# Opening loads of a two-layer SiLU kernel: the first w1 slab on one queue, the x tiles in smaller transposes

## The chip, the cores and the metric

The kernel runs on one core of one Trainium2 chip. The metric is the device time of one execution in microseconds (us); the number that counts is the median of several runs. Below, TensorE is PE in the profile (PEld is its weight load), ScalarE is ACT, VectorE is DVE, GpSimd is POOL and SyncE is SP. SP and ACT each have a queue on which they issue DMAs (SPq and ACTq).

## What is computed

`x` is 2048 x 640, `w1` is 640 x 1728, `w2` is 1728 x 640, all bf16:

```
h = silu(x @ w1)      # 2048 x 1728
out = h @ w2          # 2048 x 640
```

## The kernel before

The contraction of the first product runs over 640 = 5 tiles of 128 (`DT`, index `k`). The 1728 columns of w1 are 13 full tiles of 128 and a tail of 64 (index `ft`). The 2048 rows of x are four chunks of 512 (`SCH`, index `c`). x is brought in by DMA transposes (`turned`, line 90, and line 163), so that the contraction lies on the partitions. `xT[:, k, ...]` is contraction tile k of x, called x tile k below for chunk 0; `w1s[:, k, ...]` is the matching part of w1, and its first 1024 columns (eight tiles of 128, 256 KB) are called slab k.

A product of 128 w1 columns with 512 rows of x is issued as two matmuls of 64 columns each (`step`, line 183), which run side by side; such a pair is the unit counted below.

**Chunk 0** is ordered so that PE can begin with little data. PE takes x tile 0 with the eight column tiles of slab 0, one PSUM bank for each (eight pairs, "sweep 0"), then x tile 1 with slab 1, and so on to sweep 4, after which the eight banks are complete. Sweep k waits for slab k and x tile k (`opening`, line 197, and line 208). Then come the remaining five column tiles of chunk 0 (loads `ld_rest` and `ld_rest2`), five pairs each, and then chunks 1 to 3, each waiting for five transposes on one semaphore (`ld_xc`). The second product follows.

**Ahead of the first real matmul** PE runs matmuls on a zeroed tile `z` (`first_dummies`, line 135): thirteen of 128 columns by 256 and one pair of 64 columns by 256.

**The order of the DMAs** is written out by hand. `early` puts an instruction ahead of the kernel's opening barrier, on its engine, in the order of the calls. Before the change that order is:

- SPq: x tiles 0 and 1 in one transpose (line 123); columns 640 to 1023 of slab 0 (`ld_w1b`, line 148, 96 KB); slab 1; slab 2; x tile 2; slab 3; x tiles 3 and 4 in one transpose; slab 4; `ld_rest` (320 KB); `ld_rest2` (560 KB); then, in the body, fifteen transposes for chunks 1 to 3 and the loads of w2.
- ACTq: columns 0 to 639 of slab 0 (line 124, 160 KB), then the table load and a small activation (`warm_up`).

In sweep 0, PE waits for x tile 0 and ACT's part of slab 0, and ahead of the sixth column tile (`ft == NA`) for `ld_w1b`.

Of the kernel before, what the change touches and what calls it, by code (L numbers as in the profile page):

```python
# [9 lines left out]
def bass_standalone__dense_activation_silu__prompt_kernel(  # L10
# [13 lines left out]
    P = 128  # L24
    NB = 8
    BANK = 512
    DT = D // P
    FT = F // P
    FL = F - FT * P
    SCH = 512  # L30
# [8 lines left out]
    pe, act, dve, pool, sp = nc.tensor, nc.scalar, nc.vector, nc.gpsimd, nc.sync  # L39

    with ExitStack() as es:
# [18 lines left out]
        def sem(name):  # L60
            s = es.enter_context(nc.semaphore(name))
            count[s.name if hasattr(s, "name") else name] = 0
            return [s, 0]

        def tick(ins, s, n=1):
            ins.then_inc(s[0], n)
            s[1] += n
            return (s, s[1])

        def wait(eng, *points):  # L70
            for pt in points:
                if pt is None:
                    continue
                s, v = pt
                key = (id(eng), id(s))
                if seen.get(key, 0) < v:
                    eng.wait_ge(s[0], v)
                    seen[key] = v
# [6 lines left out]
        def load(eng, out_ap, in_ap):  # L85
            s = sem(f"s_ld{n_dma[0]}")
            n_dma[0] += 1
            return tick(eng.dma_start(out=out_ap, in_=in_ap), s, 16)

        def turned(c0, c1, k0, k1):  # L90
            s = sem(f"s_tr{n_dma[0]}")
            n_dma[0] += 1
            return tick(sp.dma_start_transpose(
                out=xT[:, k0:k1, c0:c1], in_=xf[c0:c1, k0 * P:k1 * P]), s, 16)

        ET = mybir.EngineType

        def early(emit, engine, arrived=True):
            n = len(nc.main_func.blocks[0].instructions)
            r = emit()  # L100
            lst = nc.main_func.blocks[0].instructions
            new = lst[n:]
            del lst[n:]
            at = next(
                i for i, ins in enumerate(lst)
                if ins.opcode == ("EventSemaphore" if arrived else "Drain") and ins.engine == engine
            )
            lst[at:at] = new
            return r
# [2 lines left out]
        w2_v = w2[0:F0, :].rearrange("(ft p) d -> p ft d", p=P)  # L112

        NO = NB
        NA = 5
        CO = NO * P

        def slab(eng, k, f0=0, f1=NO):
            return load(eng, w1s[:, k, f0 * P:f1 * P], w1_v[:, k, f0 * P:f1 * P])

        ld_w1 = {}
        ld_t = {}
        ld_t[0] = ld_t[1] = early(lambda: turned(0, SCH, 0, 2), ET.SP, False)
        ld_w1[0] = early(lambda: slab(act, 0, 0, NA), ET.Activation, False)
        p_z = early(lambda: tick(dve.memset(z[:, :], 0.0), s_dve), ET.DVE, False)  # L125

        bank_free = [None] * NB
# [1 line left out]
        def dummies(n, w):  # L129
            for _ in range(n):  # L130
                for c0 in range(0, P, w):
                    pe.matmul(ps[c0:c0 + w, 3, 0:HB], lhsT=z[:, 0:w], rhs=z[:, :],  # L132
                              start=True, stop=True)

        def first_dummies():
            wait(pe, p_z)
            dummies(13, P)
            dummies(1, HC)

        p_warm = early(lambda: tick(pool.memset(warm[:, :], 0.0), s_pool), ET.Pool, False)  # L140
# [4 lines left out]

        early(warm_up, ET.Activation, False)

        ld_w1b = early(lambda: slab(sp, 0, NA, NO), ET.SP, False)
        ld_w1[1] = early(lambda: slab(sp, 1), ET.SP, False)
        ld_w1[2] = early(lambda: slab(sp, 2), ET.SP, False)  # L150
        ld_t[2] = early(lambda: turned(0, SCH, 2, 3), ET.SP, False)
        ld_w1[3] = early(lambda: slab(sp, 3), ET.SP, False)
        ld_t[3] = ld_t[4] = early(lambda: turned(0, SCH, 3, DT), ET.SP, False)
        ld_w1[4] = early(lambda: slab(sp, 4), ET.SP, False)
        CM = CO + 2 * P
        ld_rest = early(lambda: load(sp, w1s[:, :, CO:CM], w1_v[:, :, CO:CM]), ET.SP, False)
# [32 lines left out]
        def part(k, ft, c0, c1, start=False, stop=False):  # L189
            return step(ft, k, ft, c0, c1, start, stop)  # L190

        def sweep(k, c0, c1, *waits):
            wait(pe, *waits)
            for ft in range(NO):
                part(k, ft, c0, c1)

        def opening():
            first_dummies()
            wait(pe, ld_t[0], ld_w1[0])
            for ft in range(NO):  # L200
                if ft == NA:
                    wait(pe, ld_w1b)
                part(0, ft, 0, SCH, start=True)
            for k in range(1, DT - 1):
                sweep(k, 0, SCH, ld_w1[k], ld_t[k])

        early(opening, ET.PE)
        wait(pe, ld_w1[4], ld_t[4])
        for ft in range(NO):
# [198 lines left out]
```

## Time and profile before

| what | value |
|---|---|
| median of 3 runs | 124.7 us (124.55 to 125.05) |
| span of the profiled execution, first to last instruction | 123.8 us |
| PE busy | 121.3 us, 98% of the span |
| ACT busy | 38.8 us, 31% |
| DVE busy | 6.9 us, 6% |
| first dummy matmul, from the span's start | 0.39 us |
| first real matmul | 3.82 us |
| granted TensorE clock, mean | 1.000 |
| DMA moved | 10.42 MB, mean 84 GB/s |

The profiled execution has no separate device time on record; its span is its own time, and the runs' median lies 0.9 us above it, for what comes before the first and after the last instruction. All times inside an execution are counted from the span's start. An issue is the time in which the queue's engine hands a DMA over; a DMA has landed when its semaphore has its full count.

### The profile page before, as it was taken

Reading aid. Unit: us, or ns where it says so; the run is one execution under the profiler, and the core shown is the slowest. Engines: PE = TensorE matmul, PEld = TensorE weight load, DVE = VectorE, ACT = ScalarE, POOL = GpSimd, SP = SyncE. Lnnn points to the kernel's source line nnn. Section 1 sums busy time; section 2 is a strip of 40 time slices with the busy share of each in tenths; the row PEclk is TensorE's granted clock in tenths of the full one; section 3 lists DMA queues with packets and bytes.
Section 4 is the critical chain, followed back from the end, with each engine's and each line's share of the span. In section 5 each row is a group of like instructions: output and inputs, shape, how many; then the busy total and the mean of one; then the engine's idle time right before and its main releaser. Section 6 shows DMA issues by size and latency. Waiting matters only on the chain.

```text
span 123.8 us, 2298 instructions
## 1 busy us (share of the span) xinstructions
PE 121.3 (98%) x1056; PEld 58.9 (48%) x1057; DVE 6.9 (6%) x11; ACT 38.8 (31%) x67; POOL 0.3 (0%) x5
## 2 busy tenths in 40 slices
PE   8999999999999999999999999999999999999993
PEld 5345545545545545545544444444444444444452
DVE  0000000000000000000000022002200300222001
ACT  4000985555555555555530011001100200110110
POOL 0000000000000000000000000000000000000000
DMA  6999974554894000000000004302200220023112
GB/s 138 239 246 331 138 86 91 100 77 107 214 394 157 0 0 0 3 5 0 0 0 5 0 0 101 74 0 105 107 0 5 106 106 0 5 106 116 53 66 82
DMA packets 19625, 10.42 MB, mean 84 GB/s; under 512 B 13728, under 2 KB 19104, under 8 KB 19616
## 3 DMA queue, kind: packets, MB, share of 16 engines
q1 hardware_dynamic: 19472, 10.11, 34.1%
q10 hardware_dynamic: 144, 0.16, 0.6%
q8 instruction: 8, 0.13, 0.5%
q14 instruction: 1, 0.01, 0.0%
HBM read 4.51 MB, written 2.62 MB: 58 GB/s over the span
## 4 chain that ended last, share of the span: by engine, by line
PE 95%; DMA 3%; ACT 0%; issue 0%
PE ps L175 95%; DMA xT<-in_x_dram 3%; ACT o_sb L256 0%
## 5 line engine op out<-in xcount | busy, mean ns | idle before, releaser
L175 PE MATMUL ps<-xT,w1s 128*64 128x512 bf16 x540 | 59.6, 384 | 0.1
L175 PE MATMUL ps<-w2s,hT 64*128 64x512 bf16 (+3 forms) x376 | 46.0, 369 | 0.2 <-issue 0.2
L175 PEld LDWEIGHTS ps<-xT,w1s 128*64 128x64 bf16 x540 | 30.0, 111 | 29.6 <-issue 1.2
L179 ACT ACTIVATE hT<-ps 128x512 bf16<-128x512 f32 x52 | 30.0, 607 | 29.9 <-PE ps L175 29.9
L175 PEld LDWEIGHTS ps<-w2s,hT 64*128 64x128 bf16 (+1 forms) x377 | 21.0, 95 | 24.2 <-issue 0.2
L256 ACT CAST o_sb<-ps 128x512 bf16<-128x512 f32 (+1 forms) x9 | 5.0, 551 | 41.5 <-PE ps L175 41.5
L175 PE MATMUL ps<-hT,w2s 64*128 64x512 bf16 x104 | 11.7, 376 | 0.0
L175 PEld LDWEIGHTS ps<-hT,w2s 64*128 64x128 bf16 x104 | 5.0, 94 | 6.3 <-issue 0.4
L254 DVE CAST o_sb<-ps 128x512 bf16<-128x512 f32 (+1 forms) x8 | 5.4, 675 | 40.5 <-PE ps L175 40.5
L254 DVE CAST oT<-ps 128x512 bf16<-128x512 f32 x2 | 1.4, 692 | 74.2 <-PE ps L175 74.2
L256 ACT CAST oT<-ps 128x512 bf16<-128x512 f32 x2 | 1.2, 586 | 10.6 <-PE ps L175 10.6
L132 PE MATMUL ps<-z 128*128 128x256 bf16 (+1 forms) x15 | 3.3, 419 | 0.4 <-DVE z L125 0.4
L175 PE MATMUL ps<-w2t,hTt 64*128 64x512 bf16 (+2 forms) x17 | 2.9, 363 | 0.0
L132 PEld LDWEIGHTS ps<-z 128*128 128x128 bf16 (+1 forms) x15 | 1.9, 142 | 1.5 <-issue 0.4
L179 ACT ACTIVATE hTt<-ps 128x512 bf16<-128x512 f32 x2 | 1.2, 598 | 1.0 <-PE ps L175 1.0
L144 ACT ACT_TABLE_LOAD x1 | 1.3, 1283 | 0.5 <-issue 0.5
L175 PEld LDWEIGHTS ps<-w2t,hTt 64*128 64x128 bf16 x17 | 0.9, 94 | 1.1
L175 PE MATMUL ps<-hTt,w2t 64*128 64x512 bf16 x4 | 0.8, 376 | 0.0
L175 PEld LDWEIGHTS ps<-hTt,w2t 64*128 64x128 bf16 x4 | 0.2, 94 | 0.2
L144 ACT ACTIVATE warm<-warm 128x32 f32<-128x32 f32 x1 | 0.2, 229 | 0.0
L125 DVE MEMSET z<- 128x128 uint32 x1 | 0.2, 165 | 0.2 <-issue 0.2
L140 POOL MEMSET warm<- 128x32 f32 x1 | 0.1, 125 | 0.0
(4 smaller groups left out, 0.4 us busy)
## 6 DMA issues: line engine op xcount, KB each, us to landing
out_dram<-o_sb SPq DMA_DIRECT2D x15, 160.0 KB, 1.8
w2s<-in_w_dram SPq DMA_DIRECT2D x1, 1120.0 KB, 6.1
w1s<-in_w_dram SPq DMA_DIRECT2D x4, 256.0 KB, 4.1
w2s<-in_w_dram SPq DMA_DIRECT2D x1, 960.0 KB, 8.2
w1s<-in_w_dram SPq DMA_DIRECT2D x1, 560.0 KB, 7.0
w1s<-in_w_dram SPq DMA_DIRECT2D x1, 320.0 KB, 5.8
xT<-in_x_dram SPq DMA_TRANSPOSE x18, 3.7
w1s<-in_w_dram ACTq DMA_DIRECT2D x1, 160.0 KB, 2.7
```

What stands on the lines that cost most here:

```text
L125: p_z = early(lambda: tick(dve.memset(z[:, :], 0.0), s_dve), ET.DVE, False)
L132: pe.matmul(ps[c0:c0 + w, 3, 0:HB], lhsT=z[:, 0:w], rhs=z[:, :], start=True, stop=True)
L140: p_warm = early(lambda: tick(pool.memset(warm[:, :], 0.0), s_pool), ET.Pool, False)
L144: act.activation(out=warm[:, :], in_=warm[:, :], func=ACT.Silu)
L175: return pe.matmul(o, lhsT=l, rhs=r, start=start, stop=stop, skip_group_check=shared)
L179: r = tick(act.activation(out=out_ap, in_=in_ap, func=ACT.Silu), s_act)
L254: r = tick(dve.tensor_copy(out=out_ap, in_=in_ap), s_dve)
L256: r = tick(act.copy(out=out_ap, in_=in_ap), s_act)
```

## The change

ACT loads the whole of slab 0, so `ld_w1b`, its wait and `NA` are gone. The first transpose on SPq brings x tile 0 alone; x tile 1 has a transpose of its own, behind slab 1, followed by that of x tile 2, which so moves ahead of slab 2. Slab 3 follows slab 2 directly; the rest keeps its order. There are eleven dummies of 128 columns instead of thirteen.

```
-        ld_t[0] = ld_t[1] = early(lambda: turned(0, SCH, 0, 2), ET.SP, False)
-        ld_w1[0] = early(lambda: slab(act, 0, 0, NA), ET.Activation, False)
+        ld_t[0] = early(lambda: turned(0, SCH, 0, 1), ET.SP, False)
+        ld_w1[0] = early(lambda: slab(act, 0), ET.Activation, False)
...
-            dummies(13, P)
+            dummies(11, P)
             dummies(1, HC)
...
-        ld_w1b = early(lambda: slab(sp, 0, NA, NO), ET.SP, False)
         ld_w1[1] = early(lambda: slab(sp, 1), ET.SP, False)
+        ld_t[1] = early(lambda: turned(0, SCH, 1, 2), ET.SP, False)
+        ld_t[2] = early(lambda: turned(0, SCH, 2, 3), ET.SP, False)
         ld_w1[2] = early(lambda: slab(sp, 2), ET.SP, False)
-        ld_t[2] = early(lambda: turned(0, SCH, 2, 3), ET.SP, False)
         ld_w1[3] = early(lambda: slab(sp, 3), ET.SP, False)
-        ld_t[3] = ld_t[4] = early(lambda: turned(0, SCH, 3, DT), ET.SP, False)
+        ld_t[3] = ld_t[4] = early(lambda: turned(0, SCH, 3, 5), ET.SP, False)
         ld_w1[4] = early(lambda: slab(sp, 4), ET.SP, False)
...
             for ft in range(NO):
-                if ft == NA:
-                    wait(pe, ld_w1b)
                 part(0, ft, 0, SCH, start=True)
```

More of the change, by code (lines that the diff above doesn't have):

```diff
@@ L114, in bass_standalone__dense_activation_silu__prompt_kernel @@
         NO = NB
-        NA = 5
         CO = NO * P
```

## The prediction

> **What bounds the kernel now.** I read the page first, then the chain of waits in order of time, then the timeline of the first 9 us, then each opening DMA by itself. The page:
>
> ```profile
> span 123.8 us, 2298 instructions
> ...
> PE 121.3 (98%) x1056; PEld 58.9 (48%) x1057; DVE 6.9 (6%) x11; ACT 38.8 (31%) x67; POOL 0.3 (0%) x5
> ...
> PE 95%; DMA 3%; ACT 0%; issue 0%
> PE ps L175 95%; DMA xT<-in_x_dram 3%; ACT o_sb L256 0%
> ```
>
> PE is the bound; the one other thing on the chain is a load of x. The chain in order of time:
>
> ```profile
> 0.00 3.78 DMA xT<-in_x_dram
> 3.78 0.04 issue
> 3.82 106.78 PE ps L175 x706
> ```
>
> The first transpose (x tiles 0 and 1) lands at 3.78, the first real matmul starts at 3.82, and from there PE is not interrupted for 106.78 us. So the change can win only by starting before 3.82, and lose only by putting a hole into what follows. The weight loads and SP's queue:
>
> ```profile
> 3.27 0.13 PEld L132 LDWEIGHTS ps<-z 128*64 128x64 bf16 x2 [0.41 <-issue]
> 3.82 0.18 PEld L175 LDWEIGHTS ps<-xT,w1s 128*64 128x64 bf16 x4 [0.42 <-DMA xT<-in_x_dram]
> 4.25 0.18 PEld L175 LDWEIGHTS ps<-xT,w1s 128*64 128x64 bf16 x2 [0.25 <-issue]
> ...
> 5.53 0.18 PEld L175 LDWEIGHTS ps<-xT,w1s 128*64 128x64 bf16 x2 [0.25 <-DMA w1s<-in_w_dram]
> 5.96 0.18 PEld L175 LDWEIGHTS ps<-xT,w1s 128*64 128x64 bf16 x2 [0.25 <-issue]
> 6.30 2.27 PEld L175 LDWEIGHTS ps<-xT,w1s 128*64 128x64 bf16 x22 [0.17 <-issue]
> ```
> ```profile
> 0.00 1.33 SPq L93 DMA_TRANSPOSE xT<-in_x_dram  x1
> 1.39 1.54 SPq L88 DMA_DIRECT2D w1s<-in_w_dram  x3
> 2.97 1.16 SPq L93 DMA_TRANSPOSE xT<-in_x_dram  x1
> 4.17 0.58 SPq L88 DMA_DIRECT2D w1s<-in_w_dram  x1
> 4.79 1.24 SPq L93 DMA_TRANSPOSE xT<-in_x_dram  x1
> 6.07 1.62 SPq L88 DMA_DIRECT2D w1s<-in_w_dram  x3
> 8.09 9.67 SPq L163 DMA_TRANSPOSE xT<-in_x_dram  x6
> ```
>
> The first rows show the pace: pairs start 0.427 apart up to 5.96, 0.34 apart once, then 0.216 (the timeline of 7 to 8 us: five pairs in 1.08). PE doubles its pace at about 6.22 (a gap of 0.343 is 0.26 us at the slow pace and the rest at the fast one), although the granted clock reads 1.00 in every stretch. The wait for the second part of slab 0 at 5.53 costs nothing: the idle 0.25 before it is that of its neighbours. Sweep 0 ends at 6.73 and each later sweep takes 8 x 0.216 = 1.73: sweeps 1 to 4 start at 6.73, 8.46, 10.19, 11.91, the remaining tiles at 13.64, chunk 1 at 13.64 + 25 x 0.216 = 19.04.
>
> **What an earlier start is worth.** A start earlier by d, with the pace doubling at the same 6.22, puts d/0.427 more pairs ahead of that point, which save 0.216 each behind it: 0.505 d. This halving is my largest choice. The trace has one doubling, 5.83 after the first dummy (0.39) and 2.40 after the first real pair; what it is tied to isn't shown. I keep it at 6.22, since PE's first dummy stays where it is; the other ties are rivals.
>
> **Part 1: when the first pair can start.**
> - x tile 0 alone: the upper bound is the two-tile transpose, 3.78. The nearest rows of one tile: 2.8 from issue to landing (the one issued at 16.49), 2.4 for the o_sb transpose from oT, 4.2 with a full queue (x tile 2). It shares its time with slab 0; I take 3.2, between 2.8 and 3.78 and nearer the lone one, as nothing is ahead of it on its queue.
> - slab 0 on ACT: issued at 0.12, the 160 KB landed 2.7 later, at 2.8. The 96 KB more, at the 248 GB/s that moved between 2 and 3 us, are 0.4: 3.2. Bounds: 2.8, and 0.12 + 3.9 = 4.0 (a 256 KB slab on SP).
> - Dummies: eleven at 0.213 (eight start from 0.39 to 1.86) end the last pair of dummies at 3.49 - 0.43 = 3.06, ahead of the data, so they hold nothing up.
>
> Start: 3.25, which is 0.57 earlier; worth 0.505 x 0.57 = **0.29 us**. Bounds of the start: 3.06 (dummies; 0.38 us) to 4.0 (0.09 us lost).
>
> **Part 2: the queue behind it.** SP loses one issue (0.61, from 1.39 to 2.00) and gains one transpose (1.20 from issue to next issue for x tile 2, 1.31 in the chain from 16.49). Going down the queue with these rows: x tile 0 at 0.00, slab 1 at 1.31, x tile 1 at 1.92, x tile 2 at 3.12, slab 2 at 4.37, slab 3 at 4.98, x tiles 3 and 4 at 5.47, slab 4 at 6.75, the rest loads at 7.37 and 7.85, chunk 1 from 8.77 (was 8.09: 0.68 later). With before's time from issue to landing for the same kind of DMA (slabs 3.9 to 4.5, x tile 2 4.2, x tiles 3 and 4 4.4, rest 5.8 and 7.0), against the need with a start at 3.25 and no hole:
>
> | needed by | need | lands by those rows |
> |---|---|---|
> | sweep 1: slab 1, x tile 1 | 6.44 | 5.2, 6.1 |
> | sweep 2: slab 2, x tile 2 | 8.17 | 8.5, 7.3 |
> | sweep 3: slab 3, x tile 3 | 9.90 | 9.1, 9.9 |
> | sweep 4: slab 4 | 11.62 | 11.25 |
> | rest, rest2 | 13.35, 15.5 | 13.2, 14.85 |
> | chunk 1 (last transpose 14.57 + 3.4 before) | 18.75 | 18.7 |
>
> Only slab 2 is late, by 0.3, in the worst reading: it was issued at 2.49 and is now at 4.37, behind both transposes. The latencies are those of a queue with a backlog. Less is ahead of it now than the rows suggest: up to slab 2 the DMAs have 896 KB to move against 864 before, but 1.9 us more to do so. Its lower bound is the 2.7 of ACT's load, 7.1; the middle of 7.1 and 8.5 is 7.8, and I take no hole. If all else fits as well, the cost of part 2 is 0, with 0.3 as its upper bound; below 0 it can't be, as PE had no hole after 3.82. ACT's longer issue is hidden: its first real activation is at 12.34. The wait removed at 5.53 was worth nothing.
>
> **Sum.** 0.29 less than the span of 123.8: 123.5, and with the 0.9 around it **124.4** (0.24% less). A measurement of this kernel can tell about 0.5%, or 0.6 us, from no change (its three runs lie 0.5 apart), so this forecast is within it.
>
> **Rivals.**
> - **A, the two loads hold each other up.** Before the first pair, 256 + 128 = 384 KB must land instead of 160 + 256 = 416. If bytes set the time, the stretch from 1.0 (first movement) to 3.78 shrinks by 32/416, 0.2 us: start 3.6, gain 0.505 x 0.2 = 0.1, 124.6. For it: the busiest early second shows 248 GB/s, well under the 347 between 10 and 11 us. Against: the transpose's small packets, now half as many, were last to land, one microsecond after slab 0's part. [...]
> - **B, the order gives it back.** Slab 2 lands at 8.5 as by the rows above: a hole of 0.3 and the gain is gone, 124.7. It would need a landing after 9.1 to lose 0.6.
> - **C, the pace doubles 2.40 after the first real pair.** Then it doubles at 5.65 and the whole 0.57 is won: 124.1. For it: 3 us of dummies had not doubled the pace. Against: there is no reason in the trace that zeros count less.
> - **D, the pace doubles later (slower).** The dummies now end at 3.06. Before, PE was idle 0.33 us (3.49 to 3.82) between them and the first pair, and the pace still doubled. If the data come after 3.4, the idle time is longer than that, and if it makes the warm-up begin anew, the 5.83 count from the first pair: with a start at 3.6, 9.43 instead of 6.22. That costs 3.21 x 0.495 less the 0.1 of A, 1.5 us: 126.2. A smaller delay costs half of itself. At a start of 3.25 the idle time is 0.19, shorter than before, which speaks against it. [...]
>
> **How the numbers follow.** Forecast 0.44, A 0.12, B 0.14, C 0.12, D 0.18. The forecast itself spreads by some 0.3 either way (the runs' spread, bounds of the start): 124.1 to 124.7. Faster by over 0.5% (below 124.1): 0.15 of the forecast, half of C and a little of the others, 0.23. Slower by over 0.5% (above 125.3): nearly all of D, and 0.06 of a hole in sweep 2 or chunk 1 beyond the rows, 0.24. Within 0.5%: 0.53. The range from 123.8 to 125.8 takes in A, B, C and the smaller delays of D, and leaves out some 0.07 below and 0.12 above.
>
> **What the profile after would show.** Right: the chain starts with a DMA that lands at 3.1 to 3.4, pairs 0.427 apart from there to about 6.2, then 0.216 with no idle time of PEld up to chunk 1. A: a start near 3.6, with slab 0 or x tile 0 named. B: an idle time before sweep 2, put down to w1s. C: the doubling near 5.65. D: slow pairs beyond 6.7, and a longer idle time ahead of the first. The prediction is wrong if x tile 0 lands no sooner than 3.7, or if the doubling moves by more than half a microsecond.

## The result and the profile after

| | before | after |
|---|---|---|
| median of 8 runs | 124.53 us (124.29 to 125.05) | 125.15 us (124.92 to 125.34) |
| ratio, 95% interval | | 1.0053 (1.0035 to 1.0071) |
| span of the profiled execution | 123.8 us | 123.7 us |
| device time of the profiled execution | not on record | 125.01 us |

The change made the kernel 0.6 us slower; a gain of 0.3 was forecast. Here and below, medians count all executions, and ratios leave out those more than 1.5% above the fastest of the same kernel.

One line of this table already shows something that the prediction missed: after, the device time lies 1.3 us above the span, not 0.9. If that holds for the kernel before as well, its profiled execution took about 125.1 us. That is the long end of its own runs: the median execution had a span of 123.2. The 0.9 was the distance from a long execution to the median, not what comes before the first and after the last instruction. So I worked from an execution that was not typical.

The page of the kernel after, the lines that answer to those of before:

```profile
span 123.7 us, 2296 instructions
...
PE 120.3 (97%) x1055; PEld 65.9 (53%) x1055; DVE 6.9 (6%) x11; ACT 38.8 (31%) x67; POOL 0.3 (0%) x5
...
PE 90%; SPq 4%; DMA 4%; issue 0%; ACT 0%
PE ps L174 90%; DMA xT<-in_x_dram 4%; SPq L93 3%; SPq L88 1%; ACT o_sb L253 0%
```

PE has one per cent less, and SP's queue, which was not on the chain before, has 4%. The chain of waits in order of time shows where (start, length, what):

```profile
0.00 1.24 SPq L93
...
1.92 1.15 SPq L93
...
3.11 1.26 SPq L93
...
5.52 4.38 DMA xT<-in_x_dram
9.89 0.14 issue
10.03 111.82 PE ps L174 x993
```

Before, the chain entered PE at 3.82. Now it stays on SP's issues, three single transposes among them, until x tiles 3 and 4 are issued at 5.52; they land at 9.89, and only from 10.03, the start of sweep 3, is PE without interruption. The weight loads of the same execution:

```profile
3.43 1.48 PEld L174 LDWEIGHTS ps<-xT,w1s 128*64 128x64 bf16 x16 [0.45 <-DMA xT<-in_x_dram]
5.83 1.47 PEld L174 LDWEIGHTS ps<-xT,w1s 128*64 128x64 bf16 x16 [0.92 <-DMA w1s<-in_w_dram]
7.60 1.44 PEld L174 LDWEIGHTS ps<-xT,w1s 128*64 128x64 bf16 x16 [0.31 <-DMA w1s<-in_w_dram]
10.00 6.00 PEld L174 LDWEIGHTS ps<-xT,w1s 128*64 128x64 bf16 x58 [0.96 <-issue]
```

Two things are to be seen. The sixteen loads (eight pairs) of sweep 0 take 1.48 us, against 3.2 at the slow pace (7 x 0.427 + 0.18): PE doubled its pace at about 3.6 here, not at 6.2. And PE then overtakes its loads. Sweep 0 ends at 5.23 (3.43 + 0.29 + 7 x 0.216), sweep 1 starts at 5.86: 0.63 us idle. Sweep 2 ends at 9.36, sweep 3 starts at 10.03: 0.67. The releaser that a row names is to be read with care. The wait ahead of sweep 1 is put down to w1s, but slab 1 had landed at 4.9 (issued at 1.30) and x tile 1 at 5.7 (1.92 + 3.8); the wait ahead of sweep 3 is put down to issue, while the chain shows x tiles 3 and 4. The table of stretches has, for 5.40 to 5.80 (after the stretch and its length: busy time and instructions of PE, PEld, DVE, ACT and POOL, then the granted clock, the DMA engines' share, GB/s), before:

```profile
5.40:5.80 0.40, 0.40 (x4) 0.18 (x2) 0.00 (x0) 0.00 (x0) 0.00 (x0) 1.00 1.36 323
```

and after:

```profile
5.40:5.80 0.40, 0.00 (x0) 0.00 (x0) 0.00 (x0) 0.00 (x0) 0.00 (x0) 1.00 0.98 110
```

Here the queue moves a third of what it moved before: SP spent 1.92 to 4.37 on two single transposes, and of slab 2, issued at 4.42, only 12 packets of 2 KB begin in this stretch, the first at 5.63; the other 83 are under 512 bytes.

**One sum for all profiles.** From the start of sweep 3 on, nearly all profiles are alike: in 19 of the 20 the span ends 113.6 to 113.7 us after it (10.19 and 123.8 before, 10.03 and 123.7 after; e3 is the exception), and the device time is 1.3 to 1.4 more. So the start of sweep 3 is the number that the experiments compare. The medians put it at 9.6 before (123.2 - 113.65) and 10.2 after.

### The profile page after: what moved, and what is told of

It is laid out like the page before. It is cut to its first block, busy times and chain, and to the rows that moved or that the text cites. A ratio compares the mean times of both kernels' runs of the same rounds, so it can differ in the third digit from the quotient of the medians.

```text
span 123.7 us, 2296 instructions
## 1 busy us (share of the span) xinstructions
PE 120.3 (97%) x1055; PEld 65.9 (53%) x1055; DVE 6.9 (6%) x11; ACT 38.8 (31%) x67; POOL 0.3 (0%) x5
## 4 chain that ended last, share of the span: by engine, by line
PE 90%; SPq 4%; DMA 4%; issue 0%; ACT 0%
PE ps L174 90%; DMA xT<-in_x_dram 4%; SPq L93 3%; SPq L88 1%; ACT o_sb L253 0%
## 5 line engine op out<-in xcount | busy, mean ns | idle before, releaser
L174 PE MATMUL ps<-xT,w1s 128*64 128x512 bf16 x540 | 58.9, 379 | 1.1 <-DMA xT<-in_x_dram 1.1
L174 PEld LDWEIGHTS ps<-xT,w1s 128*64 128x64 bf16 x540 | 37.2, 110 | 22.7 <-DMA w1s<-in_w_dram 1.2
L253 ACT CAST oT<-ps 128x512 bf16<-128x512 f32 x2 | 1.2, 586 | 10.6 <-PE ps L174 10.6
```

The source lines that it names most:

```text
L174: return pe.matmul(o, lhsT=l, rhs=r, start=start, stop=stop, skip_group_check=shared)
L253: r = tick(act.copy(out=out_ap, in_=in_ap), s_act)
```

## The experiments

**The theories.** L: the moment at which PE doubles its pace differs between executions; where it is early, the loads bound the opening, and the change brings them later. C (rival): the loss is PE's, through the shorter dummies. S (rival): slabs 2 and 3 behind the transposes are what costs. D: idle time of PE ahead of the first pair puts off the doubling. (L, C and S are not letters of the prediction, whose own C is another rival; D is the same there.) Each ratio below is to the kernel before on the same chip; e1 to e4, e5 to e8, e9 to e12, e13 to e16, and e17 and e18 ran on the chips that the record numbers 3, 6, 11, 3 and 4.

**e1, the kernel before again.** 

> The kernel before, unchanged, for a second profile. In its first profile the pace of the pairs doubled at 6.22 and the span was 123.8; the median of its eight times, 124.53, is 0.5 below that execution's. Theory L (loads): the moment of doubling differs between executions, and where it is early (3.6, as in the profile after) the loads bound the opening: span near 123.2, small idle times ahead of the sixth column tile (its part of slab 0 landed at 5.24) and nowhere later than sweep 4, first pair still at 3.8. Theory C (clock): the doubling belongs to the kernel (to the dummies and the first real pair), so this profile shows it at 6.2 again, with the span at 123.8. Ratio 1.000.

Measured: 124.38, ratio 0.998 (0.996 to 1.000); the profiled execution took 124.76 with a span of 123.4. Its weight loads:

```profile
5.14 0.18 PEld L175 LDWEIGHTS ps<-xT,w1s 128*64 128x64 bf16 x2 [0.25 <-issue]
5.56 0.46 PEld L175 LDWEIGHTS ps<-xT,w1s 128*64 128x64 bf16 x6 [0.24 <-DMA w1s<-in_w_dram]
6.21 9.75 PEld L175 LDWEIGHTS ps<-xT,w1s 128*64 128x64 bf16 x92 [0.18 <-DMA w1s<-in_w_dram]
```

The same program doubles its pace at 5.4 here, 0.8 before its first profile, and its span is 0.4 shorter. Theory C's fixed moment falls. Sweep 1 starts as slab 1 lands (6.17), so from here on an earlier doubling would have brought little. In the ten executions the span lay between 122.8 and 123.4.

**e2, x tiles 1 and 2 in one transpose.** In the changed kernel:

```
-        ld_t[1] = early(lambda: turned(0, SCH, 1, 2), ET.SP, False)
-        ld_t[2] = early(lambda: turned(0, SCH, 2, 3), ET.SP, False)
+        ld_t[1] = ld_t[2] = early(lambda: turned(0, SCH, 1, 3), ET.SP, False)
```

> The changed kernel with x tiles 1 and 2 in one transpose: one issue of about 1.2 us less on SP ahead of slabs 2, 3 and x tiles 3 and 4. Theory L: x tiles 3 and 4 are issued at 4.3 instead of 5.52 and land by 9.2 or sooner instead of 9.89; x tiles 1 and 2 land at about 6.2, so sweep 1 begins then, and two sweeps later sweep 3 near 9.7 instead of 10.03: 0.3 faster than the changed kernel, 124.8 (ratio to before 1.002). Theory S (slabs 2 and 3 behind the transposes are what costs): slab 2 is issued 1.2 earlier too, and the whole 0.6 comes back, 124.5. Theory C: dummies and start are as in the changed kernel, so 125.1.

Measured: 124.95, ratio 1.0041 (1.0015 to 1.0068). The median is 0.2 below that of the changed kernel, but the interval takes in both L's 1.002 and no return at all (1.0053); it leaves out the full return that S expected. The weight loads:

```profile
3.62 1.44 PEld L173 LDWEIGHTS ps<-xT,w1s 128*64 128x64 bf16 x16 [0.65 <-DMA xT<-in_x_dram]
6.38 1.47 PEld L173 LDWEIGHTS ps<-xT,w1s 128*64 128x64 bf16 x16 [1.31 <-issue]
8.12 1.45 PEld L173 LDWEIGHTS ps<-xT,w1s 128*64 128x64 bf16 x16 [0.28 <-DMA w1s<-in_w_dram]
9.94 6.00 PEld L173 LDWEIGHTS ps<-xT,w1s 128*64 128x64 bf16 x58 [0.37 <-issue]
```

x tiles 3 and 4 were issued at 4.31 instead of 5.52 and still landed at 9.8 (5.5 from issue to landing), so the earlier issue brought them no sooner. PE now loses a whole microsecond ahead of sweep 1, as x tiles 1 and 2 land together at 6.3, and from 6.4 it runs nearly through. One wait had taken the place of the other. S falls: slab 2 was issued 1.2 us sooner and the time did not come back.

**e3, x tile 2 behind slab 2 again.** In the changed kernel, two lines swapped:

```
-        ld_t[2] = early(lambda: turned(0, SCH, 2, 3), ET.SP, False)
         ld_w1[2] = early(lambda: slab(sp, 2), ET.SP, False)
+        ld_t[2] = early(lambda: turned(0, SCH, 2, 3), ET.SP, False)
```

> The changed kernel with the transpose of x tile 2 behind slab 2 again, as before; the number of issues ahead of x tiles 3 and 4 is the same as in the changed kernel. Theory L: x tiles 3 and 4 are issued at about 5.5 and land at about 9.9, and the time stays at 125.1 (ratio 1.005). Theory S: slab 2 lands at about 6.9 instead of 7.56, and the time comes back by 0.3 to 0.6, 124.5 to 124.8. Theory C: 125.1.

Measured: 125.15, ratio 1.0053 (1.0029 to 1.0077), as L said: slab 2 landed earlier (7.15), x tiles 3 and 4 at 9.86, as in the changed kernel. The order of x tile 2 and slab 2 is without effect on the median. The profile is of a long execution (125.78) and shows one more wait: sweep 3 started at 9.99, but the last transpose of chunk 1 landed at 19.60, and PE stood idle for 0.8 us. The prediction had left chunk 1 only 0.05 us to spare (18.75 against 18.7); in the other 19 profiles PE does not wait there.

**e4, x tiles 0 and 1 in one transpose again.** In the changed kernel:

```
-        ld_t[0] = early(lambda: turned(0, SCH, 0, 1), ET.SP, False)
+        ld_t[0] = ld_t[1] = early(lambda: turned(0, SCH, 0, 2), ET.SP, False)
...
-        ld_t[1] = early(lambda: turned(0, SCH, 1, 2), ET.SP, False)
```

> The changed kernel with x tiles 0 and 1 in one transpose at the head, as before; slab 0 stays whole on ACT, x tile 2 ahead of slab 2, eleven dummies. SP has one transpose less than in the changed kernel and one load less than before. The first pair starts at 3.8 again. Theory L: x tiles 3 and 4 are issued at about 4.35 and land at 9.0 or sooner, slab 1 lands at about 5.3, and with an early doubling the sweeps run from 3.82 with hardly an idle time: sweep 4 near 10.8, which is 0.2 to 0.3 before the kernel before and 0.9 before the changed one: 124.2 to 124.4 (ratio 0.997 to 0.999), although the first pair starts 0.4 later than in the changed kernel. Theory C (eleven dummies and a longer idle time of PE ahead of the first pair, 0.75): the doubling comes later, 125.2 or more. Theory S: x tile 2 is still ahead of slab 2, so about half of the loss stays, 124.8.

Measured: the executions fell apart into three between 124.16 and 124.72, eight between 126.11 and 126.70, and one of 259.39. The ratio of 0.9989 (0.9954 to 1.0024) is that of the first three. The profile is of one of the three (124.44):

```profile
2.85 0.13 PEld L131 LDWEIGHTS ps<-z 128*64 128x64 bf16 x2 [0.41 <-issue]
4.14 4.89 PEld L173 LDWEIGHTS ps<-xT,w1s 128*64 128x64 bf16 x48 [1.16 <-DMA xT<-in_x_dram]
9.42 6.64 PEld L173 LDWEIGHTS ps<-xT,w1s 128*64 128x64 bf16 x64 [0.39 <-issue]
```

Two things at once. Where the pace has doubled by the first pair, the loads no longer hold PE up: 48 weight loads (three sweeps) in a row, sweep 3 at 9.45, and the loss is gone though the first pair starts 0.7 later than in the changed kernel. But PE was idle for 1.08 us (3.06 to 4.14), and most executions are some 1.9 us longer, as rival D would have it; no profile is of one of these. The two effects had to be parted (e6).

**e5, the split of the first transpose alone, on the kernel before.**

```
-        ld_t[0] = ld_t[1] = early(lambda: turned(0, SCH, 0, 2), ET.SP, False)
+        ld_t[0] = early(lambda: turned(0, SCH, 0, 1), ET.SP, False)
...
         ld_w1[1] = early(lambda: slab(sp, 1), ET.SP, False)
+        ld_t[1] = early(lambda: turned(0, SCH, 1, 2), ET.SP, False)
```

> The kernel before with one part of the change alone: x tile 0 by itself at the head, x tile 1 in its own transpose behind slab 1. Slab 0 stays divided, thirteen dummies, order otherwise as before. Theory L (in executions in which the pace doubles early, the loads bound the opening, and each single transpose ahead holds SP for 1.2 us): x tile 1 lands near 6.4, x tiles 3 and 4 are issued at about 6.0 and land at about 10.3, sweep 3 begins then instead of at 9.3 to 9.5: 125.3 to 125.6 (ratio 1.006 to 1.009). Theory C (the loss is PE's clock): PE's dummies end later than x tile 0 lands, there is no idle time, the pace doubles early in every execution: 124.3 or less. If the loss were in slab 0 on ACT or in the fewer dummies: 124.5.

Measured: 125.63, ratio 1.0096 (1.0062 to 1.0130). The chain of waits:

```profile
6.04 4.42 DMA xT<-in_x_dram
10.46 0.14 issue
10.60 111.82 PE ps L176 x993
```

x tiles 3 and 4 are issued at 6.04, land at 10.46, and sweep 3 starts at 10.60. This part alone costs twice what the whole change costs; the whole change also takes `ld_w1b` off SP, 0.6 us of issue, which is about the difference between the two. Theory C, which had no idle time to blame here, falls.

**e6, e4 with fifteen dummies.** `dummies(11, P)` becomes `dummies(15, P)`. 

> The kernel of e4 (the changed one with x tiles 0 and 1 in one transpose) with fifteen dummies instead of eleven: PE is busy until 3.9 instead of 3.06, the first pair still starts at about 4.1. In e4 PE was idle for 1.08 us ahead of the first pair, and its executions fell into two groups, 124.2 to 124.7 and 126.1 to 126.7, with one of 259. [...] If the long group had another cause (a disturbed chip, the loads), it stays: most executions above 126.

Measured: 124.76, ratio 1.0016 (0.9992 to 1.0040), twelve executions from 124.44 to 125.49. The group at 126 is gone with the idle time (now 0.26 us), which bears out D for e4, though on another chip. With all twelve counted, the kernel with x tiles 0 and 1 together can't be told from the kernel before, while the whole change costs 0.53%: most of the loss sits in the split. The median is still 0.3 us above the 124.44 of the middle one of the three shorter executions of e4. x tiles 0 and 1 landed at 4.13 and slab 1 at 6.26, against 3.40 and 5.29 in e8 on the same chip, where ACT loads only a part of slab 0.

**e7, slab 2 issued by ACT.** In the changed kernel:

```
         early(warm_up, ET.Activation, False)
+        ld_w1[2] = early(lambda: slab(act, 2), ET.Activation, False)
...
-        ld_w1[2] = early(lambda: slab(sp, 2), ET.SP, False)
```

> The changed kernel with slab 2 issued by ACT, behind the table load and the small activation, at about 2.1, instead of by SP at 4.42. SP is rid of 0.6 us ahead of slab 3 and of x tiles 3 and 4. Theory L: the queue, which ran nearly empty at 5.4 to 5.8 in the changed kernel, stays full; x tiles 3 and 4 are issued at 4.9 and land at 9.0 to 9.3; x tile 1 still lands at 5.7 to 6.0, so the sweeps begin at 5.8, 7.6, 9.3: 0.6 faster than the changed kernel, 124.4 (ratio 0.999). If the DMA engines' rate alone sets the landing of x tiles 3 and 4, not SP's issue: nothing comes back, 125.1, and x tile 1 lands later, as slab 2 moves beside slab 1. Theory C: 125.1.

Measured: 124.89, ratio 1.0047 (1.0008 to 1.0085), seven executions between 124.75 and 124.89 and five between 126.15 and 127.44; the profile is of one of these five (126.15). My premise was wrong: the issue did not wait for the table load ahead of it. ACT's rows:

```profile
0.55 1.28 ACT L143 ACT_TABLE_LOAD   x1 [0.55 <-issue]
0.61 0.39 ACTq L88 DMA_DIRECT2D w1s<-in_w_dram  x1
```

So slab 2 ran beside x tile 0, which landed at 4.4 instead of 3.4, and PE was idle for 1.4 us. x tiles 3 and 4 did land sooner, at 9.2, as L said; the rest is a miss of the design and decides nothing.

**e8, eleven dummies alone, on the kernel before.** 

> The kernel before with another part of the change alone: eleven dummies instead of thirteen, nothing else. PE is idle for 0.75 us instead of 0.33 ahead of the first pair at 3.8. [...] Theory L and no threshold of the clock: 124.5 in all.

Measured: 124.68, ratio 1.0000 (0.9975 to 1.0024); nine executions between 124.38 and 124.87, one of 126.27. On this chip x tiles 0 and 1 landed at 3.40 in the profile, so the idle time was 0.38 us and not 0.75. The fewer dummies cost nothing by themselves.

**e9 and e10, no dummies at all, in the kernel before and in the changed one.** The call `first_dummies()` is taken out. 

> [...] Both theories: 125.5 to 127, wide, since the moment of doubling differs. To be compared with e10: see there.

> The changed kernel without any dummy matmul. With the doubling put off, PE needs x tile 1 at 6.8, slab 2 at about 9 and x tiles 3 and 4 at about 10.8: all have landed. Theory L (the changed kernel loses because PE, early at the fast pace, overtakes its loads): here nothing is overtaken, and it is faster than e9, by 0.2 (half of the 0.4 by which it starts earlier) to 0.4. If the loss had a cause that does not hang on PE's pace (chunk 1, a longer drain, a slower pace), it is slower than e9 by 0.6, as with dummies.

Measured: 125.95 (125.13 to 126.77), ratio 1.0106 (1.0068 to 1.0144), and 126.16 (125.46 to 126.66), ratio 1.0119 (1.0084 to 1.0155), of six executions each. The difference is lost in the scatter, and the test of sign stays open. The two profiles say more: neither has idle time of PE behind its first pair (3.55 and 3.56). The pace doubled at 6.4 in e9 and at 8.1 in e10, and 1.7 us at half pace are 0.86; the spans, 123.8 and 124.6, differ by 0.8. At the slow pace, the loads of the changed kernel cost nothing.

**e11, the changed kernel with thirteen dummies.** 

> The changed kernel with thirteen dummies, as before; nothing else undone. PE's dummies end at 3.49, about when the data are there, so no idle time is left ahead of the first pair. Theory L: the loads set the time, 125.1 (ratio 1.005), with the idle time ahead of sweeps 1 and 3 again where the pace doubles early, and sweep 3 at about 10.0 in any case. Theory C (the shorter dummies put off the doubling and cost the 0.6): 124.5 or less.

Measured: 125.08, ratio 1.0030 (1.0011 to 1.0049). Without idle time ahead of the first pair more than half of the loss is still there; C falls again. In its profile x tiles 3 and 4 landed at 9.63 and sweep 3 started at 9.77.

**e12, a version meant to beat both.** In the changed kernel:

```
-        ld_w1[1] = early(lambda: slab(sp, 1), ET.SP, False)
         ld_t[1] = early(lambda: turned(0, SCH, 1, 2), ET.SP, False)
+        ld_w1[1] = early(lambda: slab(sp, 1), ET.SP, False)
         ld_t[2] = early(lambda: turned(0, SCH, 2, 3), ET.SP, False)
-        ld_w1[2] = early(lambda: slab(sp, 2), ET.SP, False)
-        ld_w1[3] = early(lambda: slab(sp, 3), ET.SP, False)
         ld_t[3] = ld_t[4] = early(lambda: turned(0, SCH, 3, 5), ET.SP, False)
+        def late_slabs():
+            wait(act, ld_t[0])
+            ld_w1[2] = slab(act, 2)
+            ld_w1[3] = slab(act, 3)
+        early(late_slabs, ET.Activation, False)
```

and twelve dummies. 

> A version meant to beat both: x tiles 0 and 1 as two transposes at the head of SP, then slab 1, x tile 2, x tiles 3 and 4, slab 4; ACT loads slab 0, and slabs 2 and 3 once x tile 0 has landed (a wait on ACT, behind which nothing is due before 12); twelve dummies. Theory L: the first pair starts at 3.4 to 3.6, x tile 1 is there by 4.5, slab 1 (issued at 2.5) by 5.3, x tiles 3 and 4 (issued at 4.4) by 8.7: sweeps at 3.5, 5.3, 7.0, 8.8, 10.5, which is 1.2 before the changed kernel and 0.6 before the kernel before: 123.9 (ratio 0.995). If the DMA engines' rate alone sets the landing of x tiles 3 and 4 (9.2 or later): 124.4 (ratio 0.999).

Measured: a clear miss, 126.75 (124.83 to 127.16); the ratio of the five shortest of the twelve is 1.009 (1.0059 to 1.0121). The profile is of one of the seven longer ones. x tile 0 landed only at 4.2, with the next transpose right behind it, and x tiles 3 and 4, issued at 4.4 beside slabs 2 and 3 on the other queue, took 7.3 us, to 11.6. The stretch from 8 to 10 us in this kernel:

```profile
8.00:10.00 2.00, 2.00 (x20) 1.00 (x18) 0.00 (x0) 0.00 (x0) 0.00 (x0) 1.00 1.03 134
```

and in e18, the kernel before with two dummies more:

```profile
8.00:10.00 2.00, 2.00 (x22) 1.05 (x20) 0.00 (x0) 0.00 (x0) 0.00 (x0) 1.00 1.07 287
```

The same share of busy DMA engines moves less than half. The two stretches do not carry the same: 357 of 444 packets are under 512 bytes in e12, 206 of 861 in e18. So how much of this is the two queues side by side and how much the smaller packets is not shown.

**e13, the changed kernel again.** 

> The changed kernel, unchanged, on the chip of the next three, for a second profile. Theory L: whatever the moment of doubling in this profile, sweep 3 starts at 9.8 to 10.1, when x tiles 3 and 4 have landed, and the span is 123.6 to 124.0; ratio to before 1.004 to 1.006.

Measured: 125.23, ratio 1.0057 (1.0034 to 1.0079), from 124.82 to 126.33. The profile is of the longest:

```profile
3.81 0.18 PEld L174 LDWEIGHTS ps<-xT,w1s 128*64 128x64 bf16 x4 [0.83 <-DMA xT<-in_x_dram]
...
8.08 0.18 PEld L174 LDWEIGHTS ps<-xT,w1s 128*64 128x64 bf16 x2 [0.24 <-issue]
8.51 7.51 PEld L174 LDWEIGHTS ps<-xT,w1s 128*64 128x64 bf16 x70 [0.24 <-issue]
```

Not as expected: x tile 0 landed at 3.77, PE was idle for 0.75 us, the pace doubled at 8.6, and sweep 3 started at 11.4 with no wait for a load. Three of the twelve executions are above 125.6. So D touches the changed kernel too, but not its median: the other nine lie between 124.82 and 125.32.

**e14 and e17, x tile 1 directly behind x tile 0, in its own transpose.** In the changed kernel, and in e17 with fifteen dummies:

```
-        ld_w1[1] = early(lambda: slab(sp, 1), ET.SP, False)
         ld_t[1] = early(lambda: turned(0, SCH, 1, 2), ET.SP, False)
+        ld_w1[1] = early(lambda: slab(sp, 1), ET.SP, False)
```

> The changed kernel with the transpose of x tile 1 directly behind that of x tile 0, ahead of slab 1. As many issues on SP ahead of x tiles 3 and 4 as in the changed kernel, which are issued at 5.5 again. If SP's issue time is the cause (three single transposes ahead of x tiles 3 and 4): these land at about 9.8 as in the changed kernel, and the time stays at 1.005. If the place of x tile 1 behind slab 1 is the cause (sweep 1 waits for it, and the engines switch between transposes and copies once more): x tile 1 lands by 4.7, sweep 1 waits for slab 1 alone, and the time is that of the kernel before, 0.999 to 1.001.

> The kernel of e14 (x tile 1 in its own transpose directly behind that of x tile 0) with fifteen dummies, which end at 3.9, so that PE has next to no idle time ahead of the first pair at about 4.1; in e14 that idle time was 1.05 us and the pace doubled only at 9.0, which hid what the loads do. With an early doubling: if SP's issue time of the third single transpose is the cause, x tiles 3 and 4 (issued at 5.5) land at about 9.7, sweep 3 waits for them, and the time is 125.0 (ratio 1.004); if the place of x tile 1 is the cause, 124.5 (ratio 1.000).

e14 could not tell: x tile 0 landed at 4.07, PE was idle for 1.05 us, the pace doubled at 9.1 (126.05, ratio 1.0107, 1.0057 to 1.0156). e17 could: 125.18, ratio 1.0046 (1.0028 to 1.0063), all twelve between 124.91 and 125.52. Its weight loads:

```profile
6.05 0.18 PEld L174 LDWEIGHTS ps<-xT,w1s 128*64 128x64 bf16 x2 [0.25 <-issue]
6.41 3.56 PEld L174 LDWEIGHTS ps<-xT,w1s 128*64 128x64 bf16 x34 [0.18 <-issue]
10.32 5.78 PEld L174 LDWEIGHTS ps<-xT,w1s 128*64 128x64 bf16 x56 [0.35 <-issue]
```

x tile 1 was there by 5.2 and no longer in the way; x tiles 3 and 4, issued at 5.48 behind three single transposes, landed at 10.2, and sweep 3 began at 10.35. In this profile the doubling came so late (6.33) that PE lost only 0.06 us by the wait; but with that landing, an earlier doubling could not have helped. The medians show it: none of the twelve executions is below 124.91, while e18, which has the order of before on the same chip, reaches down to 123.93. So the split keeps its loss with x tile 1 out of the way.

**e15 and e16, x tiles 2 to 4 in one transpose** behind slab 2, in the kernel before (shown) and in that of e6:

```
-        ld_t[2] = early(lambda: turned(0, SCH, 2, 3), ET.SP, False)
+        ld_t[2] = ld_t[3] = ld_t[4] = early(lambda: turned(0, SCH, 2, DT), ET.SP, False)
...
-        ld_t[3] = ld_t[4] = early(lambda: turned(0, SCH, 3, DT), ET.SP, False)
```

> The kernel before with x tiles 2, 3 and 4 in one transpose behind slab 2, then slabs 3 and 4: one issue of 1.2 us less, the queue changes between transposes and copies twice instead of three times. x tile 2 lands later, 7.7 to 8.0 instead of 7.15, x tiles 3 and 4 sooner, 8.0 instead of 9.24, slab 3 at 8.7, slab 4 at 9.4. If issue time and x tiles 3 and 4 bound the kernel before too: sweep 3 starts up to 0.2 sooner, ratio 0.997 to 1.000. If x tile 2 takes their place: 1.000 to 1.002.

> The kernel of e6 (slab 0 whole on ACT, x tiles 0 and 1 in one transpose, fifteen dummies) with the same merging: x tiles 0 and 1; slab 1; slab 2; x tiles 2 to 4; slab 3; slab 4. Five issues on SP up to slab 3 instead of seven in the changed kernel. First pair at 4.1, sweep 1 at 5.85, x tiles 2 to 4 at 7.2 to 7.6, slab 3 at 8.2: sweeps 2 and 3 at 7.6 and 9.3 with an early doubling. Theory L: 0.995 to 0.998. If the rate of the engines alone counts: 1.000.

Measured: 124.94, ratio 1.0036 (1.0018 to 1.0054), and 125.18, ratio 1.0052 (1.0029 to 1.0074). Both slower: the three tiles land together at 8.1 and 8.3, and sweep 2 waits for them. The larger transpose saved an issue of 1.2 us and held back its first tile: in the kernel before, x tile 2 landed at 7.2 (2.97 + 4.2).

**e18, the kernel before with fifteen dummies.** 

> The kernel before with fifteen dummies instead of thirteen: they end at 3.92, about when x tiles 0 and 1 land, so PE has no idle time ahead of the first pair, which may start up to 0.1 later. Theory D, with a threshold above before's 0.33 us of idle time: the moment of doubling is as scattered as before, 124.5 to 124.6 (ratio 1.000 to 1.001). If any idle time puts off the doubling: the late executions of the kernel before (124.9 to 125.2) go, median 124.3 (ratio 0.998).

Measured: 124.68, ratio 0.9998 (0.9973 to 1.0023), from 123.93 to 125.30. The idle time of 0.33 us in the kernel before does no harm; the scatter is as wide as before, and I put it down to the doubling itself. No version beat the kernel before.

**What is shown and what is not.** The loss is in the split of the first transpose: e5 has the split alone and loses; in e6, and in the three shorter executions of e4, it is undone and the loss is gone or too small to tell. What it does shows in the landing of x tiles 3 and 4, which sweep 3 waits for. With the first transpose as before they land at 8.4 to 9.5 (seven profiles: before, e1, e4, e6, e8, e9, e18). With the split, and slabs 2 and 3 on SP, they land at 9.6 to 10.5 (nine: after, e2, e3, e5, e10, e11, e13, e14, e17). In the kernel after, x tile 1 also arrives behind slab 1, at 5.7, while PE at the fast pace wants it at 5.2.

How much each of the two waits is worth is not shown. e17 took the wait for x tile 1 away and kept 0.46%. e2 took away the added issue of 1.2 us, but brought x tile 1 later still (6.3), and x tiles 3 and 4 no sooner (9.8). So issue time is not all that sets their landing, and why they land so late in e2 stays open. The test that the loss vanishes when the pace doubles late rests on profiles (e10, e13), not on medians. And in the three profiles with x tile 0 alone, eleven dummies and at most 0.56 us of idle time (after, e2, e3) the pace has doubled by about 3.6, sooner than in the ten others with dummies and little idle time; whether the change itself brings this about is not shown.

## Why the prediction failed

- **The step that failed: "I keep it at 6.22".** The doubling was taken for fixed and read from one execution, which was among the longest. Over the thirteen profiles with dummies and at most 0.6 us of idle time behind them it lay between 3.6 (after) and 6.3 (e17). With a doubling at 3.6, sweeps 1 to 3 want their data at 5.2, 7.0 and 8.7, while the table of needs had 6.4, 8.2 and 9.9. The landings there were nearly right: 4.9 and 5.7 (rows 5.2 and 6.1) for sweep 1, 7.6 (taken 7.8) for slab 2, 9.9 (9.9) for x tiles 3 and 4, 10.6 (11.25) for slab 4. The zero that was left for sweep 3 was the warning. So the loads bound the opening: PE lost 0.63 and 0.67 us ahead of sweeps 1 and 3, and sweep 3 started at 10.03, against 9.6 in the median execution of before. The rivals C and D put the doubling at other moments, and neither lets it scatter from one execution to the next.
- **"The 0.9 around it"** was 1.3. The 0.9 put the sum onto the median of before, but hid that the execution which gave the 6.22 lies some 0.6 above that median. So the gain was worked out for a late doubling, and set off from a time that goes with an earlier one.
- **Part 1** was right in kind and too large in size: the first pair moved from 3.82 to 3.43 (forecast 3.25). x tile 0 landed at 3.4 and slab 0 at 2.9. Other runs gave 3.77 for x tile 0 alone (e13) and 3.4 to 3.5 for both tiles together (e8, e9, e18), so the lead is no sure thing. It was worth nothing where the pace doubled early, as sweep 3 then waits for its load.
- **"I take no hole", and rival B.** The issue times were right to 0.1 us, and B was the right mechanism with the wrong wait and price. B named slab 2 and a hole of 0.3; the holes were 0.63 ahead of sweep 1 and 0.67 ahead of sweep 3. The prediction's 896 against 864 KB up to slab 2 leave out what ACT loads; with slab 0 it is 1152 against 1024. Slab 2 landed at 7.6 all the same. B expected the gain to be used up; the loss was 0.6 because the kernel before starts sweep 3 at 9.6 in its median execution, not at 10.19.
- **Part 2, the wait for `ld_w1b` "was worth nothing"**, and with the doubling at 5.4 too: in e1 the row at 5.56 has 0.24 us, the idle time of its neighbours.
- **D** is real, at a larger idle time than forecast: with 0.75 us and more the pace doubled at 7.5 to 9.1 in four of five profiles (e7, e12, e13, e14; e4's was the exception). It stretched single executions of the changed kernel, not its median. The 1.5 us that D gave stand beside 1.9 between the two groups of e4, but where D counted 5.83 from the first pair to the doubling, it was 3.1 to 5.0 in those four profiles. That PE stays at half pace for a set time, as the numbers expected of e9 and e10 take it, no run shows: without dummies the pace doubled 2.9 (e9) and 4.5 us (e10) after the first pair. The prediction's **C** fell: in the kernel after, the pace doubled 0.15 us after the first pair and not 2.40. **A** is half right in its number (first pairs at 3.43 to 3.8 on the chips, where it gave 3.6), but it was x tile 0 that came last, 0.5 us behind slab 0. Its mechanism is borne out: on one chip x tile 0 landed at 3.17 beside the 160 KB that ACT loads in e5 and at 4.40 beside slab 0 and slab 2 in e7.

## What to carry to other kernels

Look at where the profiled execution stands among the runs before a sum is made against it, and take the moment at which the pace doubles as a spread (3.6 to 6.3 here), not as a fixed point: work out the needs for its early end, where the loads bind, as well as for its late end. The transpose that was split in two here to get its first half sooner cost SP a second issue of 1.2 us, which everything behind it on the queue paid (in e5 sweep 3 started at 10.60); count such an issue up to the last transfer that the opening waits for, and look where that lands, as an earlier issue did not land earlier in e2 (issued at 4.31 instead of 5.52, landed at 9.8 against 9.9). And where two waits stand side by side, undoing one shows little: undo both before you judge either.

## What the runs showed that was not expected

- A transpose of two tiles took SP hardly longer than one (mostly 1.24 to 1.33 us against 1.12 to 1.26).
- Transposes on SP beside plain loads on ACT's queue were slow in e12: x tiles 3 and 4 took 7.3 us from issue to landing, against 4.0 to 4.4 on the same chip with slabs 2 and 3 on SP (e9 to e11).
- Two single transposes in a row did not bring the first one sooner: on one chip x tile 0 landed at 4.2 (e12), against 3.5 where a plain load followed it (e10, e11), and on another at 4.1 (e14) against 3.8 (e13).
- ACT's table load did not hold up the DMA issued behind it in e7: the issue starts at 0.61, while the load runs from 0.55 to 1.83.
- The granted clock reads 1.00 in stretches in which the pairs run at half pace (before, 4 to 6 us: pairs 0.427 apart); the spacing of the pairs and of their weight loads shows it.
- In one execution of e4 the time was 259.4 us, about twice the usual. A pace that never doubles would not do by itself: the 117 us of PE's work behind the first pair in e4's profile would take about 231 (117 x 0.427 / 0.216), which by this estimate makes some 237 in all. No profile was taken of it, and the cause stays open.
